# A LayerNorm, attention and MLP block on one core: the MLP's matmuls cut into 32-row pieces, one row group after another

## The chip, the cores and the metric

One core of a Trainium2 chip runs the whole kernel. The metric is the device time of one execution in microseconds (us): the median of three runs before the change is 1019.53 us (1019.48 to 1019.62). The core has a matrix engine (TensorE, PE in the profile, its weight loads PEld), a vector engine (VectorE, DVE), a scalar engine (ScalarE, ACT), GpSimd (POOL) and SyncE (SP), which issues most DMA transfers. Matmuls write into PSUM, here eight banks of 128 x 512 float32. Each engine works through its own queue in order and waits for others on semaphores.

## The reference, cut to what matters

```python
xn = _layernorm(x)                               # x: 2048 x 448
q = (xn @ wq).reshape(B, S, 16, 28)              # 16 heads of 28
k, v = xn @ wk, xn @ wv                          # one head of keys and values for all
p = softmax(einsum("bhqd,bkd->bhqk", q, k) * 28 ** -0.5)
o = einsum("bhqk,bkd->bhqd", p, v) @ wo
y = max(xn @ w1, 0) @ w2                         # w1: 448 x 1792
return x + o + y
```

Everything is float32. A product is made of rounded high parts and the remainders (low parts), three matmuls for each step of the contraction.

## The kernel before

The 2048 rows of x are four blocks of 512 (`QB`). The first stage, up to 61.72 us, normalizes and transposes x, projects queries, keys and values, and stores the queries to DRAM (`qscr`). At its end SyncE stores the last block's queries, reads v back in eight gathers into `vt`, after GpSimd's memset of it (L431, L436), and loads queries (L428).

**The MLP stage** (61.72 to 386.90 us) runs over seven parts of 256 hidden columns and the four blocks. A part and a block make two up tiles (`up`, 11 matmuls of 128 rows by 128 x 512 columns into one bank, L559) and four down tiles (`down`, 6 matmuls of 128 by 128 x 448, L573): 56 up and 112 down tiles. An up tile ends with a relu on ScalarE (`hH`, L562) and a remainder on VectorE (`hL`, L563), a down tile with VectorE adding the bank to `acc` (L579). `load_part` brings a part's weights by four DMAs of SyncE (L180 to L223), and `split_part` makes high and low parts of them on GpSimd in two passes of 1920 columns (L232, L233).

**The maxima.** A softmax needs an upper bound of each row's scores. For each of 16 units of work `u` (a block of queries and four heads) `max_mm` makes 64 score tiles of 128 queries by 512 keys with the high parts alone (L470), and VectorE takes each tile's maximum (L473): 1024 in all. A head has 28 dimensions, so such a matmul takes only 32 rows of the array; four heads lie in four row groups, whose matmuls run side by side into four banks. `max_rows` later transposes a unit's maxima and puts them into the query tile by four DMAs (L495).

**The attention stage** runs from there to the end. `burst` issues the score matmuls of some (mostly four) heads' key blocks, three per score tile (L528), with maxima of later units ahead and behind; ScalarE takes the exponential (L531), `pv` multiplies by v (L596), and `o_proj` tiles (L636) add the output projection.

What sets the order is the text `ORDER`, written out by hand: `F11,3` begins the next MLP tile in bank 3 with 11 steps, `B0.0011223..5612073` is a burst of no scores with maxima on the row groups 0, 0, 1, 1, 2, 2, 3 in the banks named, `V1` a multiplication by v, `R0` a call of `max_rows` with bank 0. So in the MLP stage whole-array matmuls alternate with 53 bursts of maxima, 344 in all, and 680 maxima follow in the attention stage.

Of the kernel before, what the change touches and what calls it, by code (L numbers as in the profile page):

```python
# [17 lines left out]
NU = NQB * NHG  # L18
P_BUFS = 24

# [6 lines left out]

ORDER = """
    F11,3 F6,4 B0.0011223..5612073 f5 F11,5 F6,6 B0.0011223..1207345 f5 F6,1 F6,2 F6,0 F3,7
    B0.002233..345612 f3 F11,0 F5,3 B0.0011233..4561270 f6 F6,4 F6,5 F6,6 F4,1 B0.023..270 v3456 f2 F5,2  # L30
    B0.0012233..3457601 f6 F11,3 F6,4 F3,5 B0.0112233..7601234 f3 F6,7 F6,6 F11,0 F3,1 B0.001123..234576
    f8 F6,0 F6,2 F3,3 B0.0112233..4576102 f3 F6,4 F11,5 F5,7 B0.002233..610234 f6 F6,5 F6,6 F6,1 F3,0
    B0.0011223..2347561 f3 F11,2 F8,3 B0.0011233..4756102 f3 F6,4 F6,7 F6,5 F6,6 F5,1 R0
    B0.001123..234756 f6 F9,0 B0.002233..234756 f2 F6,1 F6,2 F6,3 F6,4 F2,7 B0.112233..560123 f9 F7,4
    B0.0011233..5601237 f4 F6,5 F6,6 F6,0 F6,1 F1,2 B0.001123..374560 f10 F6,1 B0.0012233..3745602 f5
    F6,3 F6,7 F6,4 F3,5 B0.001133..602137 f3 F11,4 F5,6 B0.0112233..0213754 f6 F6,0 F6,2 F6,1 F6,3 F3,7
    B0.0012233..5460213 f8 F10,5 B0.002233..460213 f1 F6,7 F6,4 F6,6 F6,0 F4,2 B0.0011223..1357460 f7
    F11,1 F6,3 B0.001123..574602 F6,1 F6,3 F6,5 F6,7 B0.0011233..4602135 f5 F11,4 F6,6 F3,0
    B0.0012233..2135746 f3 F6,2 F6,1 F9,3 B0.001123..574602 f2 F11,1 F6,5 B0.001133..746023 F6,1 F6,5
    F6,7 F6,4 B0.0112233..6023157 f5 F11,6 F3,0 B0.001123..231574 f3 F6,6 F6,2 F6,3 F7,1  # L40
    B0.0011223..5740623 f4 F11,5 F6,7 F6,4 F3,0 B0.0011233..6231574 f3 F6,6 F11,2 F8,3
    B0.0112233..1574062 f3 F6,1 F6,5 F6,7 F5,4 B0.001123..062315 f1 F11,7 F7,0 B0.0012233..6231547 f4
    F6,6 F6,2 F6,3 F6,1 F4,5 B0.0112233..4706231 f7 F9,4 B0.001123..706231 f2 F6,5 F6,7 F6,0 F6,6 F2,2
    B0.002233..314570 f9 F7,6 B0.0012233..3145702 f4 F6,3 F6,1 F6,4 F5,5 B0.001123..702631 f1 F11,4 F7,7
    B0.0112233..0263154 f4 F6,0 F6,2 F6,6 F6,3 F4,1 B0.0112233..5470263 f7 F11,5 F6,4 F6,7 F3,0
    B0.0011233..2631547 f3 F6,2 F11,6 F5,3 B0.0011223..1547026 f6 F6,1 F6,5 F6,4 F6,7 B0.112233..026315
    F11,4 F8,7 B0.0112233..0263154 f3 F6,0 F6,2 F6,6 F5,3 B0.002233..154702 f1 F11,6 F8,1
    B0.0112233..5470236 f3 F6,5 F6,4 F6,7 F6,0 F3,2 B0.001123..361547 f8 F6,0 B0.001123..361547 f5 F6,2
    F6,3 F4,6 B0.112233..154702 f2 F6,3 F11,1 F6,5 B0.0011223..4702631 f5 F6,4 F6,7 F6,0 F4,2
    B0.112233..631547 f2 F6,0 F6,6 F6,3 F6,1 B6.223..547206317 B7.022.013.5240635143210 V1  # L50
    B4.3.02.6514032 V1 B4.13.0.4635210 V1 B4.3.12.6453021 V1 B4.13.2.3624150 V1 B3.00.0.634201 V1
    B4.2.01.5630412 V1 B5.13.011.3516204536 R1 V1 B4.123..5230461 V1 B3.000..253406 V1 B4.3.12.1250364
    V1 B4.3.02.0162453 V1 B4.03.1.2051364 V1 B6.23.2.201543612 V1 B3.11.1.054236 V1 B3.00.0.150346 V1
    B4.1.23.2154063 V1 B4.13.0.1265340 R2 V1 r B4.3.12.1560342 V2 B4.13.2.0145263 V1 n B4.2.01.1054326
    V1 B4.3.12.5120643 V1 B4.3.12.0541326 V1 B4.3.02.1025643 V1 B4.3.12.5140326 V1 B4.3.02.0521643 V1
    B4.3.12.1045326 V1 B4.03.2.5120643 V1 B4.00.3.5102364 V1 B4.03.2.5130426 V1 B4.13.2.5103642 V1
    B4.23.1.1530264 R3 V1 B4.3.12.1054263 V1 r B4.3.01.4160352 V1 B4.3.02.0415623 V1 n B4.3.12.5024316
    V1 B4.3.01.4510623 V1 B4.23.0.0425316 V1 B4.13.2.2054631 V1 B4.23.0.0245163 R4 V1 B4.3.01.0523164 V1
    B4.23.0.3065421 V1 B4.02.1.6350142 V1 B4.23.0.6350214 R5 V1 B4.3.01.6034215 V1 B5.2.12.46105321 V1
    B3.02.1.462015 V1 B4.12.0.3462051 V1 B4.13.2.4362105 V1 r B4.23.1.3426510 V1 B4.3.01.2364051 V1 n  # L60
    B4.03.1.4253160 V1 B4.12.0.4235016 V1 B4.12.0.2435601 V1 B4.22.3.4235160 V1 B4.3.01.3412506 V1
    B4.3.02.2304615 V1 B4.3.01.4213506 V1 B4.3.02.3402615 V1 B4.03.2.2314506 V1 B4.3.02.2341650 V1
    B4.2.01.1253046 V1 B4.03.12.51426305 V1 B4.13.0.2140653 V1 B4.02.1.1204365 V1 r B4.13.2.1204536 V1
    B4.3.01.2140653 V1 n B4.23.1.0251346 V1 B4.13.2.5012634 V1 B4.12.0.0521463 R5 V1 B4.3.01.0213465 V1
    B4.3.01.3062514 V1 B4.3.02.2310465 V1 B4.3.12.0263514 V1 B4.02.1.3012465 V1 B4.2.01.3012546 V1
    B4.02.1.1340625 V1 B4.3.01.1340652 V1 B4.03.1.0153246 V1 B4.11.00.01356241 V1 B4.3.02.6034512 V1 r
    B4.3.12.4610235 V1 B4.03.2.0436512 V1 n B4.1.0.046325 O12,1 B4.3.02.4056321 V1 B4.13.2.6420153 V1
    B4.02.1.4602315 V2 B4.13.2.4602531 R6 V1 B4.2.01.4201536 V1 B4.13.2.0432615 V1 B4.03.1.4023561 V1
    B4.23.0.4032156 R3 V1 B4.2.01.4206153 V1 B4.3.02.0452361 V1 B4.03.1.2064153 V1 B4.0.1.204631 O12,5
    O5,2 r B4.02..014635 f7 O2,0 B4.1.0.146352 f10 n B4.13.2.4126350 V2 B4.012..1462035 V2  # L70
    B4.23.1.1240635 V1 B4.02.1.4102563 V1 B4.23.0.4102356 V1 B4.3.12.0421635 V1 B4.13.2.1034526 V1
    B4.03.2.0143652 V1 B4.12.0.0134265 V1 B4.13.2.1034526 V1 B4.23.1.0143652 V1 B4.3.01.4031265 R1 V1
    B4.2.01.4605321 V2 B4.12.0.0426153 V1 B4.3.02.4026315 r V1 B4.2.01.6410523 V1 B4.13.2.1624305 V1 n
    B4.3.12.6142530 V1 B4.3.02.2631045 V1 B4.3.02.1246530 V1 B4.3.12.6132045 V1 B4.13.2.2641530 V1
    B4.3.12.6214503 V1 B4.3.02.4602135 V1 B4.3.01.2436501 V1 B4.3.02.6204135 V1 B4.3.12.4632501 V1
    B4.03.1.2406135 V1 B4.11.3.2460513 V1 B4.03.2.4256301 V1 B4.23.1.4265130 R6 V1 r B4.2.01.4520136 V1
    B4.23.1.2435601 V1 n B4.03.2.3254160 V1 B4.13.0.3245016 V1 B4.03.1.2354601 V1 B4.00.3.2345160 V1
    B4.12.0.2314056 V1 B4.1.0.321460 V1 B4.1.0.523014 V1 B4.3.02.6254301 V1 B4.2.01.4602153 V1
    B4.13.2.0456321 V1 B4.2.01.4065312 V1 B4.12.3.6410253 V1 B4.3.01.4610325 V1 B4.23.0.0426513 V1 r
    B4.2.01.2064351 V1 B4.12.0.6250143 R2 V1 n B4.3.01.6503142 V1 B4.13.2.3645201 V1 B4.3.02.6354120 V1  # L80
    B4.3.02.4623051 V1 B4.3.01.3456120 V1 B4.23.1.6324051 V1 B4.3.12.2643105 V1 B4.13.2.3206541 V1
    B4.2.01.2360154 V1 B4.23.0.6253401 V1 B4.13.2.5632140 V1 B4.1.0.652301 V1 B4.0.2.456123 O12,0 O7,4 r
    B4.0.1.536120 f5 O11,5 n B4.01..306124 f1 O6,3 B4.1.0.601524 f6 B4.3.02.0641523 V2 B4.23.0.1026345
    V1 B4.1.0.216053 V2 B4.123..4123605 V1 B4.3.01.1426305 V1 B4.3.01.6104253 V2 B4.23.0.4651302 V1
    B4.13.2.5416230 V1 B4.13.2.4561023 V1 B4.13.0.5416302 V1 B4.23.1.4561230 V1 B4.1.0.641502 V1
    B4.13.0.3462150 V1 B4.23.0.4326015 V1 B4.13.0.2463501 V1 r B4.3.01.4236150 V1 B4.3.12.6452031 V1 n
# [17 lines left out]
def attention_plus_mlp(ctx: ExitStack, tc: tile.TileContext, x, wq, wk, wv, wo, w1, w2, out):  # L104
# [293 lines left out]
    for b in range(1, NQB):  # L398
# [12 lines left out]
        if b == 2:  # L411
            split_part(0, g0)
# [347 lines left out]
```

## Time and profile before

| what | us |
|---|---|
| median of three runs | 1019.53 |
| the profiled execution, its own time | 1021.57 |
| its span | 1019.8 |
| MLP stage in it | 325.2 |
| VectorE's busy time in the MLP stage | 306.1 |
| first MLP matmul | 61.72 |
| last matmul of the MLP | 386.9 |

A profile's row gives the start and length in us, or for groups the count, busy time, mean length in ns and idle time before; names before the arrow are written, names behind it are read. A matmul's length includes the time until its result is in PSUM, so matmuls overlap, and the pace is read from starts. `L559` is line 559 of the kernel before. In the changed kernel the lines are others: L672 for MLP matmuls, L545 for maxima.

### The profile page before, as it was taken

Reading aid. Unit: us, or ns where it says so; the run is one execution under the profiler, and the core shown is the slowest. Engines: PE = TensorE matmul, PEld = TensorE weight load, DVE = VectorE, ACT = ScalarE, POOL = GpSimd, SP = SyncE. Lnnn points to the kernel's source line nnn. Section 1 sums busy time; section 2 is a strip of 40 time slices with the busy share of each in tenths; the row PEclk is TensorE's granted clock in tenths of the full one; section 3 lists DMA queues with packets and bytes.
Section 4 is the critical chain, followed back from the end, with each engine's and each line's share of the span. In section 5 each row is a group of like instructions: output and inputs, shape, how many; then the busy total and the mean of one; then the engine's idle time right before and its main releaser. Section 6 shows DMA issues by size and latency. Waiting matters only on the chain.

```text
span 1019.8 us, 20214 instructions
## 1 busy us (share of the span) xinstructions
PE 1012.6 (99%) x7964; PEld 602.2 (59%) x7964; DVE 800.0 (78%) x1383; ACT 606.4 (59%) x1185; POOL 114.7 (11%) x109
## 2 busy tenths in 40 slices
PE   9999999999999999999999999999999999999998
PEld 8787777777778775444444455444446444446444
DVE  7659999999999998888788876888886787785402
ACT  5531011100011006888989987889987899897994
POOL 4302202020210002011011011010111010110110
PEclk9999999999999998999999999999999999999999
DMA  7653010100200001001001102000101011000001
GB/s 244 246 168 107 1 50 1 50 1 15 74 1 11 1 11 33 33 13 44 23 23 33 33 22 71 22 23 29 37 14 59 21 33 33 2 13 29 22 13 37
DMA packets 28354, 43.22 MB, mean 42 GB/s; under 512 B 9140, under 2 KB 20084, under 8 KB 28260
## 3 DMA queue, kind: packets, MB, share of 16 engines
q1 hardware_dynamic: 27972, 41.48, 12.6%
q8 instruction: 62, 1.02, 0.4%
q10 hardware_dynamic: 288, 0.46, 0.1%
q14 instruction: 32, 0.26, 0.1%
HBM read 29.36 MB, written 12.18 MB: 41 GB/s over the span
## 4 chain that ended last, share of the span: by engine, by line
PE 97%; DVE 2%; DMA 1%; ACT 0%; SPq 0%; issue 0%; DVEq 0%; ACTq 0%
PE o L596 25%; PE b L528 24%; PE b L559 13%; PE b L573 12%; PE b L470 10%; PE b L636 4%; PE b L346 3%; PE o L559 2%; PE o L573 2%; DVE nmx L473 1%; PE b L355 1%; PE b L295 1%; PE b L324 0%; PE o L470 0%; DMA acc<-in_A_x 0%; DMA d<-oS 0%
## 5 line engine op out<-in xcount | busy, mean ns | idle before, releaser
L473 DVE TENSOR_REDUCE nmx<-b 128x1 f32<-128x512 f32 x980 | 617.6, 684 | 116.1 <-PE b L470 99.6
L531 ACT ACTIVATE p<-b 128x512 f32<-128x512 f32 x1023 | 527.7, 608 | 94.1 <-PE b L528 90.1
L528 PE MATMUL b<-q,kHL 28*128 28x512 f32 x3069 | 341.3, 427 | 0.5 <-DVE nmx L473 0.5
L528 PEld LDWEIGHTS b<-q,kHL 28*128 28x128 f32 x3069 | 202.2, 183 | 182.6 <-DVE nmx L473 129.6
L470 PE MATMUL b<-kHL,qhi 28*128 28x512 f32 x980 | 271.7, 467 | 0.1
L596 PE MATMUL o<-p,vtile 128*32 128x512 f32 x2048 | 269.7, 606 | 0.0
L562 ACT ACTIVATE hH<-b 128x512 fp32r<-128x512 f32 x49 | 29.4, 599 | 230.2 <-PE b L559 214.8
L470 PEld LDWEIGHTS b<-kHL,qhi 28*128 28x128 f32 x980 | 120.4, 183 | 77.0 <-DVE nmx L473 30.1
L559 PE MATMUL b<-xt,w 128*128 128x512 f32 x539 | 135.7, 397 | 0.0
L559 PEld LDWEIGHTS b<-xt,w 128*128 128x128 f32 x539 | 98.8, 188 | 28.1 <-issue 9.1
L573 PE MATMUL b<-w,hH 128*128 128x448 f32 x396 | 114.5, 369 | 0.0
L596 PEld LDWEIGHTS o<-p,vtile 128*32 128x32 f32 x2048 | 42.6, 108 | 74.2 <-issue 68.2
L573 PEld LDWEIGHTS b<-w,hH 128*128 128x128 f32 x396 | 73.2, 188 | 11.3 <-issue 2.9
L620 POOL TENSOR_TENSOR on<-rb,oS 128x512 f32<-128x512 f32 x15 | 19.3, 1285 | 535.3 <-DMA rb<-rscr 431.3
L573 PE MATMUL b<-w,hL 128*128 128x448 f32 x198 | 72.7, 367 | 0.0
L579 DVE TENSOR_TENSOR acc<-b,acc 128x448 f32<-128x448 f32 x99 | 56.8, 613 | 0.8 <-PE b L573 0.6
L573 PEld LDWEIGHTS b<-w,hL 128*128 128x128 f32 x198 | 37.2, 188 | 3.8 <-issue 0.9
L641 DVE TENSOR_TENSOR acc<-b,acc 128x448 f32<-128x448 f32 x16 | 10.0, 624 | 36.7 <-PE b L636 36.6
L563 DVE SCALAR_TENSOR_TENSOR hL<-b,hH 128x512 fp32r<-128x512 f32 x49 | 33.0, 681 | 3.1 <-ACT hH L562 2.9
L232 POOL TENSOR_SCALAR w<-stg 128x1920 fp32r<-128x1920 f32 x7 | 12.6, 1804 | 190.8 <-PE b L573 144.7
L346 PE MATMUL b<-xt,w 128*128 128x512 f32 x132 | 31.2, 391 | 0.0
L233 POOL TENSOR_TENSOR w<-stg,w 128x1920 fp32r<-128x1920 f32 x7 | 30.3, 4328 | 0.6
(107 smaller groups left out, 520.1 us busy)
## 6 DMA issues: line engine op xcount, KB each, us to landing
qscr<-qs SPq DMA_DIRECT2D x16, 512.0 KB
q<-qscr SPq DMA_DIRECT2D x16, 512.0 KB
qhi<-qscr SPq DMA_DIRECT2D x16, 256.0 KB
rb<-rscr SPq DMA_DIRECT2D x60, 64.0 KB
out<-acc SPq DMA_DIRECT2D x16, 224.0 KB
acc<-in_A_x SPq DMA_DIRECT2D x14, 224.0 KB
stg<-in_B_w SPq DMA_DIRECT2D x7, 448.0 KB
stg<-in_B_w SPq DMA_DIRECT2D x7, 384.0 KB
```

Source lines behind the costliest of these rows:

```text
L233: nc.gpsimd.tensor_tensor(wt[:, 1, 0:n], g[:, 0:n], wt[:, 0, 0:n].bitcast(F32), op=ALU.subtract)
L346: nc.tensor.matmul(pq, w, xm, start=n == 0, stop=n == len(steps) - 1)
L470: nc.tensor.matmul(pm, qhi[u][rows, s * P : (s + 1) * P], kHL[rows, h, 0], start=True, stop=True)
L473: nc.vector.tensor_reduce(nmx[u][:, r, s, h : h + 1], pm, axis=AX.X, op=ALU.max)
L528: nc.tensor.matmul(ps[r], kHL[rows, kt, w, keys], qst[u][rows, s, :], start=k == 0, stop=k == 2)
L531: nc.scalar.activation(p, ps[r], AF.Exp, scale=SCALE)
L559: nc.tensor.matmul(ph, w, xm, start=i == 0, stop=i == len(steps) - 1)
L563: nc.vector.scalar_tensor_tensor(hL[:, f], ph, 0.0, hH[:, f].bitcast(F32), op0=ALU.max, op1=ALU.subtract)
L573: nc.tensor.matmul(py[:, 0:D], hm[:, i * P : (i + 1) * P], wm, start=k == 0, stop=k == len(steps) - 1)
L579: nc.vector.tensor_tensor(acc[:, t, :], py[:, 0:D], acc[:, t, :], op=ALU.add)
L596: nc.tensor.matmul(o_acc[u][RB * j : RB * (j + 1)], vtile[:, kb, :], ps[j], start=kb == 0, stop=kb == NKB - 1)
L636: nc.tensor.matmul(py[:, 0:D], om[:, i * P : (i + 1) * P], wm, start=n == 0, stop=n == len(steps) - 1)
```

## The change

The whole contraction of an MLP tile is cut by rows: `Tile.passes(r)` lists the pieces of row group `r` (32 of 128 partitions), 11 or 10 for an up tile (the last chunk of xn's low part needs no second pass on row groups 2 and 3), 6 for a down tile. All four row groups add into the same bank, one after the other. Between two visits stands a hop: the last matmul of a visit is awaited by an instruction on SyncE (`nc.sync.nop()`), and the first matmul of the next visit waits for that one.

So that the row groups work side by side, several tiles are open at once, each visited by another row group. A new text, `ROWS`, gives the order matmul by matmul: a digit is the next matmul of that row group, `a` to `d` open a tile, `e` to `h` take up an open one, `i` to `l` are single maxima, `m` to `p` with `q` to `t` are pairs of maxima, `v` pops a piece of VectorE's work. `ORDER` is left with the attention stage.

Further parts: in a pair, the second matmul takes `kD`, the difference of two key blocks, ScalarE takes its relu into `more`, and VectorE adds the first tile and takes the maximum of both in one pass (`max_combine`). A down tile ends with a ScalarE copy into `y` and a GpSimd addition to `acc`. `split_part` works in six pieces, one per tile begun. `v_rows` transposes v into one bank. The MLP stage makes 426 maxima now (292 single, 67 pairs), the attention stage 598. Its 250 bursts have 22 without maxima where there were 11.

The core of the diff; the order texts are shown by one line:

```diff
-    F11,3 F6,4 B0.0011223..5612073 f5 F11,5 F6,6 B0.0011223..1207345 f5 F6,1 F6,2 F6,0 F3,7
+    a3b4c5012012012012012d6012301230123012313o7m23s1q03f53e41g33012012012vA012012l1vA012012l0012vAp7012
...
+    class Tile:
+        def __init__(self, kind, n, i, b):
...
+            if kind == "U" and i == 0:
+                if blk == 1 and 1 <= p < NPART - 1:
+                    raw[p + 1] = load_part(p + 1)
+                if blk == 2 and p < NPART - 1:
+                    splits.append(split_part(p + 1, raw.pop(p + 1)))
+            if splits and next(splits[0], True):
+                splits.pop()
...
+        def matmuls(self, r):
+            o = self.ps if self.kind == "U" else self.ps[:, 0:D]
+            steps = self.passes(r)
+            for k, (w, m) in enumerate(steps):
+                self.left -= 1
+                mm = nc.tensor.matmul(o, w, m, start=self.left == self.n_mm - 1, stop=self.left == 0)
+                if k == 0 and self.before:
+                    tc.add_manual_dep(mm.ins, self.before, HOP, reason="the row group before is done")
+                if k + 1 == len(steps) and self.left:
+                    seen = nc.sync.nop()
+                    tc.add_manual_dep(seen.ins, mm.ins.name, HOP, reason="the row group is done")
+                    self.before = seen.ins.name
                 yield
...
-        t = blk * TPB + i
-        nc.vector.tensor_tensor(acc[:, t, :], py[:, 0:D], acc[:, t, :], op=ALU.add)
-        yield
...
+            a = acc[:, blk * TPB + self.i, :]
+            y = dpool.tile([P, D], F32, name="y", bufs=4)
+            nc.scalar.activation(y, self.ps[:, 0:D], AF.Copy)
+            nc.gpsimd.tensor_tensor(a, y, a, op=ALU.add)
...
+    def max_combine(u, pm, dst, more):
+        nc.vector.tensor_tensor_reduce(more, pm, more, 1.0, LEAST, ALU.add, ALU.max, dst)
+        n_max[u] += 2
...
+    def owe_combine(a, d):
+        more = dpool.tile([P, QB], F32, name="more")
+        nc.scalar.activation(more, d[1], AF.Relu)
```

TensorE before, at the MLP's first burst (xt and w are the MLP's operands, kHL and qhi the keys and queries of the maxima, b0 to b6 and o the eight banks):

```order
L559 MATMUL b3_783<-xt_198,w_631 128x512 x9
L559 MATMUL b4_797<-xt_198,w_631 128x512 [waits PE_49]
L559 MATMUL b4_797<-xt_198,w_631 128x512 x5
L470 MATMUL b5_805<-kHL_76,qhi_681 128x512 [waits DMAHW7_49,PE_49]
L470 MATMUL b6_808<-kHL_76,qhi_681 128x512
L470 MATMUL b1_811<-kHL_76,qhi_681 128x512 [waits DVE_49]
L470 MATMUL b2_814<-kHL_76,qhi_681 128x512 [waits DVE_49]
L470 MATMUL b0_817<-kHL_76,qhi_681 128x512
L470 MATMUL o_820<-kHL_76,qhi_681 128x512
L470 MATMUL b3_823<-kHL_76,qhi_681 128x512 [waits DVE_49]
L559 MATMUL b4_797<-xt_198,w_631 128x512 x5
```

Whole tiles stand in a row, and seven maxima stand together between two parts of a tile.

TensorE now, at the first hops; the first of these rows is the 38th matmul of the MLP stage (kD is the difference of key blocks):

```order
L672 MATMUL b6_812<-xt_353,w_633 128x512
L545 MATMUL o_838<-kHL_76,qhi_687 128x512 [waits DMAHW7_49]
L545 MATMUL b2_840<-kHL_76,qhi_687 128x512 [waits DVE_49]
L672 MATMUL b6_812<-xt_353,w_633 128x512
L545 MATMUL b1_843<-kD_77,qhi_687 128x512
L545 MATMUL b0_847<-kD_77,qhi_687 128x512
L672 MATMUL b6_812<-xt_353,w_633 128x512
L672 MATMUL b5_795<-xt_353,w_633 128x512 [waits SP_sequencer_49]
L672 MATMUL b6_812<-xt_353,w_633 128x512
L672 MATMUL b4_793<-xt_199,w_633 128x512 [waits SP_sequencer_49]
L672 MATMUL b5_795<-xt_353,w_633 128x512
L672 MATMUL b3_791<-xt_199,w_633 128x512
```

Pieces of four tiles alternate, the maxima stand singly between them, and a tile taken up by its next row group (b5, b4) waits for SyncE.

SyncE before, from the last stores of the first stage on (stg is the staging tile of the MLP's weights):

```order
L334 DMA qscr<-qs 128x1024 x4
L436 DMA q<-qscr 16x1x1024
L436 DMA q<-qscr 12x1x1024
...
L428 DMA q<-qscr 128x1024 x4
L180 DMA stg<-in_B_w 128x3x256
L181 DMA stg<-in_B_w 64x256
L182 DMA stg<-in_B_w 64x256
L223 DMA stg<-in_B_w 128x2x448
L369 DMA qhi<-qscr 128x512
```

SyncE now at the same place; the waiting instructions of the hops are not printed:

```order
L405 DMA qscr<-qs 128x1024 x4
L512 DMA q<-qscr 16x1x1024
L512 DMA q<-qscr 12x1x1024
...
L504 DMA q<-qscr 128x1024 x3
L246 DMA stg<-in_B_w 128x3x256
L247 DMA stg<-in_B_w 64x256
L248 DMA stg<-in_B_w 64x256
L289 DMA stg<-in_B_w 128x2x448
L440 DMA qhi<-qscr 128x512
```

The transfers are the same but for one query load, which comes later. The first 75 hops stand between L504 and L246, behind the gathers and the query loads, and the others stand among the transfers that follow.

More of the change, by code (lines that the diff above doesn't have):

```diff
@@ L467, in max_mm, with max_reduce, max_final @@
             nmx[u] = small.tile([P, HG, TPB, 4], F32, name="nmx", bufs=3)
+            nc.vector.memset(nmx[u], LEAST)
         pm = bank(b)
         rows = slice(RB * r, RB * r + DH)
-        nc.tensor.matmul(
-            pm, qhi[u][rows, s * P : (s + 1) * P], kHL[rows, h, 0], start=True, stop=True
-        )
-        nc.vector.tensor_reduce(nmx[u][:, r, s, h : h + 1], pm, axis=AX.X, op=ALU.max)
-        if any(k and k[0][0] == u for k in todo.values()):
-            return
+        k = kD[rows, h // 2] if keys is kD else kHL[rows, h, 0]
+        nc.tensor.matmul(pm, qhi[u][rows, s * P : (s + 1) * P], k, start=True, stop=True)
+        return u, pm, nmx[u][:, r, s, h : h + 1]
+    def max_reduce(u, pm, dst):
+        nc.vector.tensor_reduce(dst, pm, axis=AX.X, op=ALU.max)
+        n_max[u] += 1
+    def max_combine(u, pm, dst, more):
+        nc.vector.tensor_tensor_reduce(more, pm, more, 1.0, LEAST, ALU.add, ALU.max, dst)
+        n_max[u] += 2
+    def max_final(u):
         nm = small.tile([P, HG, 1, TPB], F32, name="nm")
@@ L566, in down @@
-    def down(n, i, b):
-        p, blk = tasks[n]
-        hH, hL = hid[n]
-        w = parts[p][1]
-        py = bank(b)
-        steps = [(hm[:, f], w[:, wi, f, :]) for f in range(FC) for hm, wi in ((hH, 0), (hH, 1), (hL, 0))]
-        for k, (hm, wm) in enumerate(steps):
-            nc.tensor.matmul(
-                py[:, 0:D], hm[:, i * P : (i + 1) * P], wm, start=k == 0, stop=k == len(steps) - 1
-            )
-            if k + 1 < len(steps):
-                yield
-        t = blk * TPB + i
-        nc.vector.tensor_tensor(acc[:, t, :], py[:, 0:D], acc[:, t, :], op=ALU.add)
-        yield
+    splits = []
@@ new lines, in attention_plus_mlp, with owe_final, owe_reduce, work @@
+    owed, at, busy, first_of = [], {}, {}, {}
+    def owe_final(u):
+        if n_max[u] == HG * TPB * 4:
+            owed.append(lambda: max_final(u))
+    def owe_reduce(*m):
+        def work():
+            max_reduce(*m)
+            owe_final(m[0])
+        owed.append(work)
+    def owe_combine(a, d):
+        more = dpool.tile([P, QB], F32, name="more")
+        nc.scalar.activation(more, d[1], AF.Relu)
+        def work():
+            max_combine(*a, more)
+            owe_final(a[0])
+        owed.append(work)
@@ new lines, in go_on @@
+    def go_on(r):
+        t, mm = busy[r]
+        next(mm)
+        if not t.left:
+            t.finish()
+    stream = iter("".join(ROWS.split()))
+    n_tiles = 0
+    for c in stream:
+        if c in "0123":
+            go_on(int(c))
+            continue
+        b = next(stream)
+        r = (ord(c) - ord("a")) % HG
+        if c in "abcd":
+            at[b] = Tile(*mlp_tiles[n_tiles], b)
+            n_tiles += 1
+        if c in "abcdefgh":
+            busy[r] = at[b], at[b].matmuls(r)
+            go_on(r)
+        elif c in "ijkl":
+            owe_reduce(*max_mm(b, r))
+        elif c in "mnop":
+            first_of[r] = max_mm(b, r)
+        elif c in "qrst":
+            owe_combine(first_of.pop(r), max_mm(b, r, kD))
+        elif c == "v":
+            owed.pop(ord(b) - ord("A"))()
+        else:
+            max_rows(b)
+            v_rows(next(stream))
```

342 lines of the change are left out of this document (209 added, 133 removed).

## The prediction

> **What bounds the kernel now.** I read the page first, then three windows (the MLP stage, the attention stage with row maxima and without), the groups of the MLP stage, and the timeline of single tiles. First the page's head:
>
> ```profile
> span 1019.8 us, 20214 instructions
> ...
> PE 1012.6 (99%) x7964; PEld 602.2 (59%) x7964; DVE 800.0 (78%) x1383; ACT 606.4 (59%) x1185; POOL 114.7 (11%) x109
> ```
>
> TensorE always has a matmul in flight, so time is won by issuing less on it or by issuing more at once. The windows (stretch, length, then busy time and count for PE, PEld, DVE, ACT, POOL, granted clock) split the span:
>
> ```profile
> 61.72:386.90 325.18, 325.18 (x1650) 257.22 (x1648) 306.08 (x527) 35.14 (x62) 39.00 (x14) 1.00 0.09 30
> 398.00:948.00 550.00, 549.36 (x5329) 258.76 (x5323) 432.56 (x716) 475.36 (x934) 45.29 (x40) 1.00 0.09 29
> 948.00:1005.00 57.00, 57.00 (x557) 26.28 (x555) 9.25 (x18) 51.12 (x102) 6.38 (x6) 1.00 0.03 7
> 375.00:400.00 25.00, 24.73 (x156) 15.96 (x153) 20.84 (x35) 9.18 (x19) 5.43 (x3) 0.86 0.15 33
> ```
>
> The MLP stage takes 325.2 us, with TensorE at 100% and VectorE at 306.1 (94%): both are full. What a tile costs there is read from the starts of TensorE's rows:
>
> ```profile
> 207.77 1.56 PE L559 MATMUL o<-xt,w 128*128 128x512 f32 x6
> 209.25 0.79 PE L470 MATMUL b<-kHL,qhi 28*128 28x512 f32 x7
> 209.97 1.42 PE L559 MATMUL o<-xt,w 128*128 128x512 f32 x5
> 211.23 2.66 PE L559 MATMUL b<-xt,w 128*128 128x512 f32 x11
> 213.73 0.57 PE L573 MATMUL b<-w,hH 128*128 128x448 f32 x2
> 214.13 0.36 PE L573 MATMUL b<-w,hL 128*128 128x448 f32 x1
> 214.34 0.36 PE L573 MATMUL b<-w,hH 128*128 128x448 f32 x1
> ```
>
> Eleven up matmuls last 213.73 - 211.23 = 2.50 us, 0.227 each; three down matmuls 214.34 - 213.73 = 0.61, 0.203 each. The stage has 56 x 11 = 616 of the first and 112 x 6 = 672 of the second: 139.8 + 136.4 = 276.2 us. The other 49.0 us go to the 53 bursts with 344 maxima that the order counts there, 0.92 each. The one above agrees: 211.23 - 207.77 = 3.46 for eleven up matmuls and a burst, 0.96 over 2.50, for seven maxima that are two rounds on four row groups. Two rounds are 0.46; the other half is the entry and exit.
>
> **The change: the lanes of the MLP stage.** With every MLP matmul cut into 32-row pieces, a row group ("lane") carries one piece of each: 616 up pieces on lanes 0 and 1 (560 on 2 and 3), 672 down pieces, and 88, 94, 124 and 120 of now 426 maxima. Lane 1 is the fullest: 710 pieces of 512 columns and 672 of 448. At the whole-array prices that is 161.2 + 136.4 = 297.6 us, the low end. For the high end, four lanes at work side by side:
>
> ```profile
> 966.23 1.92 PE L596 MATMUL o<-p,vtile 128*32 128x512 f32 x16
> 968.09 1.74 PE L528 MATMUL b<-q,kHL 28*128 28x512 f32 x21
> 969.75 0.64 PE L596 MATMUL o<-p,vtile 128*32 128x512 f32 x4
> ```
>
> 21 score matmuls put six on a lane in 969.75 - 968.09 = 1.66 us; without an entry and exit of some 0.24 (half the 0.46 above, since this is one switch) that is 0.237 a round, with its waits: 168.3 + 142.4 = 310.7. I take the middle, 0.232 and 0.207: 164.7 + 139.1 = **303.8 us**. The 53 entries and exits are gone, and maxima ride in rounds that the MLP fills.
>
> By the Trainium skill (TensorEngine Tiling (Array Packing), When to Use Tiling) row tiles are for contractions of up to 64; a contraction of 128 fills the array whole, and cutting it should win nothing. The rows above say the same of the matmuls (297.6 is 276.2 plus 94 rounds of maxima), so by rule and row the gain is only the switches.
>
> **The hops.** A group of the MLP stage (mean length 397 ns) and the first row after an up tile on ScalarE:
>
> ```profile
> L559 PE MATMUL b<-xt,w 128*128 128x512 f32 x539 | 135.7, 397 | 0.0
> ```
>
> ```profile
> 213.93 0.60 ACT L562 ACTIVATE hH<-b 128x512 fp32r<-128x512 f32 x1 [1.90 <-PE b L559]
> ```
>
> A tile has four visits, so three hops: 504 hops from TensorE over a SyncE instruction and back. Behind a visit's waiting first matmul stands, in TensorE's one queue, the work of all four lanes. A last matmul is seen 0.40 us after its start, and a waiting engine starts 0.04 after it ends (the last of the eleven, at 211.23 + 10 x 0.227 = 213.50, ends at 213.89, and the relu starts at 213.93); the weight load behind a wait adds what the first of five up matmuls lost above, 1.26 - 5 x 0.227 = 0.12. With two such handovers a hop is about 0.40 + 2 x 0.04 + 0.12 = 0.60, up to 0.70 with SyncE's own step, which no row shows. In the new order the visits of a tile stand 14 matmuls apart in the median, 13 at the first quarter, 11 at the first tenth. 5,466 matmuls in 303.8 us are 0.056 each, so 0.78, 0.72 and 0.61 us: most hops fit and about fifty are short by up to 0.1. With the lanes not quite in step I put **4 us** on both (0 to 17: the order has 1,462 greedy rounds against 1,382 on lane 1, and 80 rounds are 17).
>
> **What stands ahead of the hops on SyncE.** SyncE takes its queue in order, and its DMA issues block hops (start, length, line, what is moved):
>
> ```profile
> 54.90 8.70 SPq L334 DMA_DIRECT2D qscr<-qs  x4
> 67.15 6.42 SPq L436 DMA_DIRECT2D q<-qscr  x8
> 73.62 1.36 SPq L428 DMA_DIRECT2D q<-qscr  x3
> ...
> 138.77 2.82 SPq L495 DMA_DIRECT2D q<-rows  x4
> 141.69 0.38 SPq L180 DMA_DIRECT2D stg<-in_B_w  x1
> ...
> 143.34 0.58 SPq L223 DMA_DIRECT2D stg<-in_B_w  x1
> ```
>
> TensorE's first MLP row and GpSimd's row of that time:
>
> ```profile
> 61.72 4.01 PE L559 MATMUL b<-xt,w 128*128 128x512 f32 x17
> ```
>
> ```profile
> 66.17 0.95 POOL L431 MEMSET q<- 128x1024 f32 x1 [14.78 <-DVE hL L563]
> ```
>
> The MLP starts at 61.72, but SyncE is busy with v's eight gathers, held back by GpSimd's memset until 67.12, and three query loads until 73.62 + 1.36 = 74.98. None moves. The first hop is the 45th matmul, some twelve rounds or 2.8 us in: TensorE stands from 64.5 to 75.1, **10.5 us**, with only four maxima ahead of it. Each of five weight loads in the stage is four issues, 141.69 to 143.92 = 2.2 us; the hop behind is then ready 0.45 + 2.2 + 0.1 after its load's turn, against some 1.6 by the order (the tile's next visit stands 29 matmuls on, at 0.056): 1.1 each, **5.5**. The maxima's rows come once: 0.9 until ScalarE has copied them, 2.8 of issues and one more query load make 4.1, against 31 matmuls or 1.7 to the next hop: **2.5**. An idle TensorE also loses clock: the window 375:400, with its pauses, was granted 0.86, so 0.14 x 25 = 3.5 us were lost; for the first stall I take **2.5** (0 to 3.5).
>
> **What the other engines do.** The accumulation into acc leaves VectorE for a ScalarE copy and a GpSimd add; maxima in pairs take one ScalarE pass and one VectorE pass with a second, short instruction. Rows:
>
> ```profile
> L473 DVE TENSOR_REDUCE nmx<-b 128x1 f32<-128x512 f32 x301 | 187.5, 682 | 12.7 <-PE b L470 11.1 <-PE o L470 1.2
> L563 DVE SCALAR_TENSOR_TENSOR hL<-b,hH 128x512 fp32r<-128x512 f32 x49 | 33.0, 681 | 3.1 <-ACT hH L562 2.9
> L562 ACT ACTIVATE hH<-b 128x512 fp32r<-128x512 f32 x49 | 29.4, 599 | 230.2 <-PE b L559 214.8 <-DVE nmx L473 15.4
> L233 POOL TENSOR_TENSOR w<-stg,w 128x1920 fp32r<-128x1920 f32 x6 | 26.0, 4330 | 0.5
> L232 POOL TENSOR_SCALAR w<-stg 128x1920 fp32r<-128x1920 f32 x6 | 10.8, 1804 | 190.8 <-PE b L573 144.7 <-DMA stg<-in_B_w 46.1
> ```
>
> VectorE: 292 single maxima at 187.5/301 = 0.62, 56 hL at 33.0/49 = 0.67, 67 pairs at 0.67 plus up to 0.2 for the second instruction: 181 + 38 + 58 = 277 us, under 306. The pair's instruction is in no row; 0.67 is the nearest (PSUM and SBUF in, 512 columns), twice that is the far end (322). ScalarE: (56 + 67 + 112) x 0.60 = 141. GpSimd: 448 columns at 4.33/1920 us each are 1.0, so 112 x 1.0 + 37 for the splits (26.0 + 10.8) = 149. Both lie beside TensorE's 304 at no cost; if GpSimd fell behind, the four y buffers would hold ScalarE's copy and with it a PSUM bank. The smaller edits (kD on GpSimd, v's transposes in one bank, ksel and tmp in another pool) lie beside other work: nothing.
>
> Stage: 303.8 + 4 + 10.5 + 5.5 + 2.5 + 2.5 = 328.8 against 325.2: **+3.6 us**.
>
> **Attention.** It keeps 598 maxima instead of 680. With maxima it issues 5,329 matmuls in 550.0 us, 0.103 each; almost without, 557 in 57.0, 0.102. So one matmul less is worth 0.103: 82 x 0.103 = 8.4, the likely low end (0 if ScalarE's exponentials set the pace, which at 475 of 550 they nearly do). If each spared a round, 82 x 0.232 = 19. I take **-11**, near the first, because 22 bursts instead of 11 now have no maxima and lose a round.
>
> Sum: 3.6 - 11 = -7.4. The profiled execution took 1021.57 with a span of 1019.8; this makes it 1014.2. On the median 1019.53 it gives **1012 us**; its own range, with lanes and attention between their nearer values, is 1003 to 1020.
>
> **Rivals.**
> SyncE is not in the way (0.20): the hops are served between the DMA issues. Then 10.5 + 5.5 + 2.5 + 2.5 = 21 us fall away: 991. Against it stand the SyncE rows; for it, that the gathers' 6.4 us were measured with nothing waiting behind.
>
> Issue becomes the bound (0.22). One more row on the score bursts:
>
> ```profile
> 964.27 2.03 PE L528 MATMUL b<-q,kHL 28*128 28x512 f32 x21
> ```
>
> 5,466 weight loads and matmuls need one pair per 0.056 us for 300 us. No row shows that pace held: the 37 from 964.27 to 968.09 took 0.103 each, the best burst 1.66/21 = 0.079, both within the array's own time. For the change, the seven maxima above went in 0.72 with a switch in it. The rival decides at (325.2 + 11 - 25)/5466 = 0.057 us (25 being the 4 and 21 us of loss and stalls), just above what is needed. At 0.062, a quarter of the way from 0.056 to 0.079, the lanes take 339 instead of 308 and the kernel 1012 + 31 = 1043; at 0.079 it would be far slower. The Trainium skill (TensorE: Matmul & The Clock Gate, Wait — 56ns, not 53.3ns?) gives some 62 ns per matmul where microcode decodes, and a floor of about 25 between starts where it does not bind; by the first this rival is certain, by the second void, and no row here tells which holds.
>
> VectorE or PSUM banks hold it (0.11): at twice the price VectorE needs 322, and SyncE's 21 us of stalls come on top, 343 in the stage: +18 - 11, 1027.
>
> **How the numbers follow.** The forecast has 0.47 (0.42 of it faster). Faster by over 0.2% (2 us, about what a measurement here can tell from no change) is below 1017.5: that 0.42 and the first rival, 0.62. Within: 0.06. Slower: 0.32, the second and third rival but for 0.01. The range goes from 988 (the first rival with its lanes at the low end) to 1044.
>
> **What would show it.** In the changed profile: TensorE idle from about 64.5 to 75 with SyncE as releaser, and a clock below 1.00 after it; about 1.1 us at each weight load; otherwise rounds of 0.23 with four lanes in flight; VectorE at 85%; the MLP stage's end near 390, attention 622 us long. A first hop before 70 makes the first rival right; lane rounds over 0.24 with no releaser the second. No idle time at the first hops, or an attention stage that keeps its 633 us, would make the sum wrong.

## The result, and the profile after

The changed kernel takes 1032.28 us (median of four runs, 1030.32 to 1034.15) against 1019.58 for the kernel before on the same chip: a ratio of 1.0124, 95% interval 1.0099 to 1.015. The forecast was 1012, faster; it came out slower by 12.7 us, inside the range (988 to 1044) and on the other side of no change. The profiled execution took 1034.06 with a span of 1031.9.

The head of the page of the changed kernel:

```profile
span 1031.9 us, 28533 instructions
...
PE 1006.4 (98%) x11704; PEld 639.8 (62%) x11704; DVE 717.8 (70%) x1287; ACT 699.6 (68%) x1361; POOL 248.9 (24%) x251
```

VectorE went from 800 to 718 us busy, as meant, and TensorE still has a matmul in flight for 98% of the span. The busy share alone shows little of the loss: TensorE is busy as long as one lane of four has a matmul in flight, and a halved clock is hidden altogether. The windows show both. First the whole MLP stage, most of attention, and the stretches in which something is wrong (length, then busy time and count for PE, PEld, DVE, ACT, POOL, then the granted clock):

```profile
61.95:404.05 342.10, 323.94 (x5473) 307.00 (x5472) 268.36 (x504) 127.66 (x235) 165.66 (x147) 0.98 0.10 30
404.05:964.00 559.95, 558.19 (x5355) 253.07 (x5355) 399.12 (x662) 486.50 (x958) 53.56 (x47) 0.98 0.10 30
66.00:76.50 10.50, 0.00 (x0) 0.00 (x0) 1.31 (x4) 1.09 (x2) 0.95 (x1) 0.58 0.18 50
76.50:82.00 5.50, 5.47 (x45) 5.42 (x49) 1.38 (x2) 0.37 (x1) 2.28 (x3) 0.56 0.75 276
405.00:420.00 15.00, 14.75 (x98) 7.09 (x94) 10.66 (x18) 10.13 (x21) 7.78 (x7) 0.66 0.31 72
458.00:468.00 10.00, 8.64 (x58) 3.35 (x58) 5.95 (x10) 5.33 (x11) 3.16 (x3) 0.66 0.10 28
```

The MLP stage takes 342.1 us (325.2 before, 328.8 forecast), what follows it 1031.9 - 404.05 = 627.9 (632.9 before, 622 forecast). So both halves missed: +13.3 and +5.9. The 404.05 takes in two maxima behind the last MLP matmul, which starts at 403.52; counted to that start, as the 325.2 before is and as the stages of the experiments below are, the stage is 341.6.

Where the first stall sits is in three views. TensorE's row (start, length; in brackets the idle time and its releaser), the first behind a matmul that started at 64.84:

```profile
76.53 2.07 PE L672 MATMUL b<-xt,w 32*128 32x512 f32 x12 [11.30 <-SPq L676]
```

SyncE's DMA issues of that time, and GpSimd's rows:

```profile
55.09 8.64 SPq L405 DMA_DIRECT2D qscr<-qs  x4
68.58 6.42 SPq L512 DMA_DIRECT2D q<-qscr  x8
75.05 1.37 SPq L504 DMA_DIRECT2D q<-qscr  x3
```

```profile
59.81 1.29 POOL L484 TENSOR_TENSOR kD<-kHL 128x512 fp32r<-128x512 f32 x1 [7.41 <-ACT kHL L397]
67.61 0.95 POOL L507 MEMSET q<- 128x1024 f32 x1 [6.51 <-DMA qscr<-qs]
```

This is the mechanism of the forecast, row by row: the first hop (L676) stands behind eight gathers that wait for a memset, and three query loads, to 75.05 + 1.37 = 76.4; TensorE goes on 0.1 later. It is 11.7 us where 10.5 were forecast, because the memset, which waits for the last qscr write to land, ran 1.4 later than before (67.61 against 66.17).

Then the pace between the pauses, in windows of the MLP stage (length, TensorE busy and its count, clock, DMA share, GB/s):

```profile
61.95:100.00 38.05, 26.73 (x372) 0.82 0.21 73
100.00:125.00 25.00, 25.00 (x445) 1.00 0.01 2
125.00:150.00 25.00, 23.28 (x403) 1.00 0.18 52
150.00:175.00 25.00, 25.00 (x436) 1.00 0.01 3
175.00:200.00 25.00, 23.62 (x412) 1.00 0.17 52
200.00:225.00 25.00, 23.82 (x415) 1.00 0.10 22
225.00:250.00 25.00, 25.00 (x451) 1.00 0.08 23
250.00:275.00 25.00, 24.21 (x420) 1.00 0.17 51
275.00:300.00 25.00, 25.00 (x445) 1.00 0.01 3
300.00:325.00 25.00, 24.59 (x422) 1.00 0.17 53
325.00:350.00 25.00, 25.00 (x438) 1.00 0.01 2
350.00:375.00 25.00, 25.00 (x440) 1.00 0.04 13
375.00:404.05 29.05, 27.69 (x456) 1.00 0.06 21
```

Six windows are without a pause: 2,655 matmuls in 150 us. A matmul that lies across an edge counts in both windows (the thirteen count 5,555 for 5,473), so about 7 come off each, and a matmul takes 150/2,613 = 0.0574 us. By that pace the stage's 5,466 matmuls are 314 us, and the rest is what each window lost: 38.05 - 365 x 0.0574 = 17.1 at the start, 8.1 in the five windows with a weight load, 3.3 in the last one with the maxima's rows. 314 + 17.1 + 8.1 + 3.3 = 342.5, and 342.1 were measured. The 8.1 hold 6.5 us of pauses at the loads and two pauses of 0.8 that VectorE releases, shown next.

One load, on TensorE and on SyncE, shows what the others repeat:

```profile
127.66 0.35 PE L672 MATMUL b<-w,hL 32*128 32x448 f32 x1
129.32 0.47 PE L672 MATMUL b<-w,hH 32*128 32x448 f32 x1 [1.31 <-SPq L676]
```

```profile
126.96 0.39 SPq L246 DMA_DIRECT2D stg<-in_B_w  x1
127.40 0.54 SPq L247 DMA_DIRECT2D stg<-in_B_w  x1
127.99 0.59 SPq L248 DMA_DIRECT2D stg<-in_B_w  x1
128.62 0.59 SPq L289 DMA_DIRECT2D stg<-in_B_w  x1
```

The four issues end at 129.21, and every lane stands still until 129.32: starts 1.66 apart. The five pauses are 1.66, 1.34, 1.57, 1.15 and 0.80 us. Two more of 0.8, at 145 and 195, have VectorE as releaser, where a unit's last maxima are put together between reduces.

The groups of the other engines (busy time, mean ns of one, idle time ahead and its releasers) that answer to the costs in the forecast:

```profile
L549 DVE TENSOR_REDUCE nmx<-b 128x1 f32<-128x512 f32 x859 | 550.7, 685 | 181.4 <-PE b L545 129.5 <-PE b L612 28.5 <-PE b L672 18.5
L553 DVE CUSTOM_DVE_ANT_0 more<-b,more 128x512 f32<-128x512 f32 x55 | 37.6, 686 | 17.3 <-ACT more L714 17.0
L696 ACT ACTIVATE y<-b 128x448 f32<-128x448 f32 x98 | 52.4, 545 | 95.3 <-PE b L672 83.6 <-PE o L672 7.2 <-PE b L545 2.9
L697 POOL TENSOR_TENSOR acc<-y,acc 128x448 f32<-128x448 f32 x112 | 127.7, 1152 | 158.9 <-ACT y L696 158.5
```

A pair's pass is 0.69 us, no dearer than a single reduce; VectorE is busy for 268 of 342 us; GpSimd idles 159 us for lack of copies. None of them is full; how far they set the pace all the same, the runs below test.

### The profile page after: what moved, and what is told of

Read it like the earlier page. It is cut to its first block, busy times and chain, and to the rows that moved or that the text cites. A ratio compares the mean times of both kernels' runs of the same rounds, so it can differ in the third digit from the quotient of the medians.

```text
span 1031.9 us, 28533 instructions
## 1 busy us (share of the span) xinstructions
PE 1006.4 (98%) x11704; PEld 639.8 (62%) x11704; DVE 717.8 (70%) x1287; ACT 699.6 (68%) x1361; POOL 248.9 (24%) x251
## 3 DMA queue, kind: packets, MB, share of 16 engines
q1 hardware_dynamic: 27972, 41.48, 12.7%
## 4 chain that ended last, share of the span: by engine, by line
PE 93%; SPq 2%; DVE 2%; DMA 1%; ACT 1%; issue 1%; POOL 0%; POOLq 0%; DVEq 0%; ACTq 0%
PE b L612 24%; PE o L769 24%; PE b L672 22%; PE b L545 8%; PE b L809 4%; PE o L672 3%; PE b L417 3%; PE b L426 1%; PE b L366 1%; SPq L512 1%; DVE nmx L549 1%; PE o L545 0%; PE b L395 0%; DMA d<-oS 0%; DMA qscr<-qs 0%
## 5 line engine op out<-in xcount | busy, mean ns | idle before, releaser
L612 PE MATMUL b<-q,kHL 28*128 28x512 f32 (+1 forms) x3066 | 335.0, 429 | 1.4 <-DVE nmx L549 1.3
L612 PEld LDWEIGHTS b<-q,kHL 28*128 28x128 f32 (+1 forms) x3066 | 194.4, 185 | 198.6 <-DVE nmx L549 101.3
L672 PE MATMUL b<-xt,w 32*128 32x512 f32 x2058 | 304.2, 397 | 12.7 <-SPq L676 12.7
L672 PE MATMUL b<-w,hH 32*128 32x448 f32 x1568 | 282.2, 368 | 3.9 <-SPq L676 3.9
L672 PEld LDWEIGHTS b<-xt,w 32*128 32x128 f32 x2058 | 248.0, 185 | 15.4 <-SPq L676 13.5
L672 PE MATMUL b<-w,hL 32*128 32x448 f32 x784 | 211.3, 363 | 0.0
L672 PEld LDWEIGHTS b<-w,hH 32*128 32x128 f32 x1568 | 205.4, 183 | 8.8 <-SPq L676 5.5
L697 POOL TENSOR_TENSOR acc<-y,acc 128x448 f32<-128x448 f32 x112 | 127.7, 1152 | 158.9 <-ACT y L696 158.5
L672 PEld LDWEIGHTS b<-w,hL 32*128 32x128 f32 x784 | 123.0, 183 | 0.4
L672 PE MATMUL o<-xt,w 32*128 32x512 f32 x294 | 73.8, 391 | 0.0
```

What stands on the lines that cost most here:

```text
L612: nc.tensor.matmul(ps[r], kHL[rows, kt, w, keys], qst[u][rows, s, :], start=k == 0, stop=k == 2)
L672: mm = nc.tensor.matmul(o, w, m, start=self.left == self.n_mm - 1, stop=self.left == 0)
L697: nc.gpsimd.tensor_tensor(a, y, a, op=ALU.add)
```

## The experiments

Theory: what was lost is TensorE standing behind SyncE's queue, plus the clock that follows. Rivals: PSUM banks and VectorE; ScalarE or GpSimd; the issue of 5,466 small matmuls. All times are medians, with the ratio to the kernel before and its 95% interval.

**Gathers off SyncE.** In load_q and at the gathers (L504 to L516), with a list that the MLP loop empties:

```diff
-            nc.sync.dma_start(vt[d0 : d0 + n].rearrange("p s q -> p (s q)"), src)
-    load_q(0); load_q(1); load_q(2)
+            later.append((vt[d0 : d0 + n].rearrange("p s q -> p (s q)"), src))
...
+            if later and n_tiles % 6 == 0:
+                one_later()          # nc.scalar.dma_start of the next one
```

> Edit: v's eight gathers and the first three query loads leave SyncE's queue; each is issued by ScalarE on its own, one at every sixth tile of the MLP stage. Everything else is as in the changed kernel. Theory (SyncE's queue blocks the first hops): the stall from 64.84 to 76.53 (11.7 us) goes, and with it the half clock behind it (76.5 to 81.4 at half is 2.4 us lost) and the slow rounds of the restart: 14 to 16.5 us in all, 1032.3 to about 1017. Rival 1 (something else holds TensorE there, PSUM banks or VectorE's hL): no more than 4 us, 1028 to 1033. Rival 2 (a DMA issue on ScalarE holds a PSUM bank as long as it held a hop on SyncE): eleven times about 0.5 us come back, 1021 to 1023.

Measured: 1019.19, ratio 0.9993 (0.9973 to 1.0013). The 11.7 us pause is gone and the kernel 13 faster than changed: the theory's side. In the profile the stage is 8.5 shorter (333.1 against 341.6), not 14 to 16.5: the clock is still at half twice inside the stage, 3.4 us each (from 69.5 and from 380.1), and 1.4 us of pause stay at 66.2, released by a pair's ScalarE copy, which itself waited:

```profile
66.90 1.09 ACT L721 ACTIVATE more<-b 128x512 f32<-128x512 f32 x2 [4.31 <-DMA qscr<-qs]
```

**Loads off SyncE.** In load_part:

```diff
+        by = nc.scalar if p > 1 else nc.sync
-            nc.sync.dma_start(...)   # four of them
+            by.dma_start(...)
```

> Edit: the five weight loads of the MLP stage (four DMAs each) are issued by ScalarE instead of SyncE; the rest is as in the changed kernel, the stall at the start too. Theory (the issues hold the hop behind them): the pauses of 1.66, 1.34, 1.57, 1.15 and 0.80 us and the rounds lost around them go, 6 to 8 us of 1032.3: about 1025. Rival (the pauses come from GpSimd's splits of the weights or from a late ScalarE copy, not from SyncE): 1031 to 1034.

Measured: 1032.0, ratio 1.0119 (1.0099 to 1.0138): no gain. The time went to the rival's side, and its profile says why. ScalarE and TensorE at the same load:

```profile
127.91 0.60 ACT L688 ACTIVATE hH<-b 128x512 fp32r<-128x512 f32 x1 [0.68 <-PE b L673]
127.92 0.39 ACTq L246 DMA_DIRECT2D stg<-in_B_w  x1
...
129.56 0.60 ACTq L290 DMA_DIRECT2D stg<-in_B_w  x1
130.21 0.60 ACT L688 ACTIVATE hH<-b 128x512 fp32r<-128x512 f32 x1 [1.70 <-PE b L546]
130.70 0.98 ACT L697 ACTIVATE y<-b 128x448 f32<-128x448 f32 x2
131.29 0.50 PE L546 MATMUL b<-kHL,qhi 28*128 28x512 f32 x1 [1.06 <-ACT y L697]
```

The same 2.2 us of issue now shut ScalarE, whose copies free the PSUM banks, and TensorE waits for a bank (ACT y) instead of a hop. The stall was moved.

**All of the stage's DMAs off SyncE.** Both edits, and in load_qhi and max_rows:

```diff
-            nc.sync.dma_start(qhi[u].bitcast(F32), queries(u)[:, 0])
+            mlp_q[0].dma_start(qhi[u].bitcast(F32), queries(u)[:, 0])   # nc.scalar in the MLP stage
```

> Edit: both of the edits before, and the queries' loads and the maxima's four row DMAs of the MLP stage are ScalarE's too: SyncE has nothing but hops between the start and the end of the stage. Theory: the start's 14 to 16.5, the loads' 6 to 8 and some 2 us at the maxima's rows add up, 1032.3 - 25 = about 1007 (1004 to 1011), below the kernel before (1019.5). Rival (lanes, banks or VectorE hold the stage, and the stalls hid their lateness): no more than half of it, 1018 or above.

Measured: 1021.67, ratio 1.0018 (1.0003 to 1.0033): the start's gain and nothing more, and the theory's 1007 missed. At the maxima's rows the pause grew from 1.75 to 2.84 us, for the reason just seen.

**No reduces in the MLP stage.**

```diff
-            max_reduce(*m)
+            n_max[m[0]] += 1
...
-        nc.scalar.activation(more, d[1], AF.Relu)
-            max_combine(*a, more)
+            n_max[a[0]] += 2
```

> Edit: the row maxima of the MLP stage keep their matmuls, but are not reduced: 292 single reduces, 67 ScalarE copies and 67 pair instructions are left out (a constant stands in for those maxima). SyncE's stalls stay. Theory (lanes and order set the pace between the stalls: 1,462 rounds, 0.057 us per matmul): the stage stays at 335 to 342 us, the kernel 1025 to 1032. Rival (VectorE, or PSUM banks that it frees late, set the pace): the stage falls to lane 1's 297.6 plus some 25 us of stalls, 323, the kernel to about 1013.

Measured: 1028.63, ratio 1.0073 (1.0047 to 1.0099); the stage 336.9, of 335 to 342 forecast by the theory. VectorE costs 4.7 us of the stage (341.6 to 336.9), the two pauses at its final maxima among them; it is not the bound. Between the pauses a matmul takes 0.0564 us here (five windows of 25 us with 2,252 matmuls, less 7 each), against 0.0574.

**One issue at a time.** As the first experiment, and:

```diff
+    spread = []      # load_part and unit 0's max_rows append their four DMAs here
...
             n_tiles += 1
+            if spread:
+                nc.scalar.dma_start(*spread.pop(0))
```

> Edit: as e1_start, and the four DMAs of each weight load and the four row DMAs of the maxima are no longer issued in one go: ScalarE issues one of them per tile. Theory (what costs is a queue, SyncE's or ScalarE's, that is shut for 2.2 us at a stretch; a single issue of 0.4 to 0.6 us fits into the slack of a PSUM bank): of the 6.5 us lost around the five loads some 5 go and 2 at the maxima's rows, e1_start's 1019.2 to about 1012 (1010 to 1015). Rival (any issue on an engine that frees banks costs its own length, however it is spaced): 1018 to 1020, as e1_start.

Measured: 1011.61, ratio 0.9914 (0.989 to 0.9937): faster than the kernel before by 0.86%, and than the first experiment by 7.6 us. The same work, on the same engine as in the second experiment, one issue per tile instead of four in a row, costs next to nothing in the windows:

```profile
100.00:125.00 25.00, 25.00 (x445) 24.32 (x443) 21.92 (x40) 9.19 (x17) 10.27 (x9) 1.00 0.15 44
200.00:225.00 25.00, 25.00 (x452) 24.26 (x448) 20.63 (x38) 9.71 (x18) 14.16 (x14) 1.00 0.27 84
```

Both windows hold a weight load or other spread transfers (DMA shares 0.15 and 0.27) and run at the pace of the pause-free ones; the five others with such transfers hold 429 to 438 matmuls, where the changed kernel's pause-free ones hold 436 to 451. The stage is 322.9. Single executions at a clock of 1.000 say the same as the medians: 1014.75 for the first experiment, 1007.12 for this one.

**One issue at a time on SyncE.** The first experiment with nc.sync in place of nc.scalar in its edit.

> Edit: as e1_start, the eight gathers and three query loads one at every sixth tile, but issued by SyncE, between its hops. Theory (a hop takes about 0.6 us and its distance is 0.78 in the median, so 0.8 us of issue ahead of it is late by some 0.5): 8 x 0.6 + 3 x 0.2 = 5 us over e1_start's 1019.2, 1023 to 1025. Rival (single issues hide between the hops; only the lump of 7.9 us behind a late memset hurt): 1019 to 1020.

Measured: 1020.0, ratio 0.9997 (0.9981 to 1.0013), the same as on ScalarE (1019.19), stage 331.5. My theory of a 0.5 us loss per issue falls: a single issue of up to 0.8 us hides between hops. What hurt was the lump. Only the gathers and query loads were spread on SyncE; the weight loads were not.

**The clock.** The changed kernel again, unedited.

> The changed kernel once more, unedited, for its own times beside the granted clock of each execution. Theory (the halved clock is part of the loss, in pieces of 3.4 us that depend on when a pause falls): times from 1028 to 1035, lower where the clock is higher, by about 10 us for 0.01 of clock, and 1016 to 1018 when carried on to a clock of 1.00. Rival (the differences have another cause): no such line.

Measured: 1030.73, ratio 1.0105 (1.0089 to 1.0122); four executions from 1030.49 to 1032.32 at clocks of 0.988 to 0.986. Too narrow to draw a line by itself; the first experiment's ten executions draw it: 1014.75 at a clock of 1.000, 1016.46 at 0.998, 1018.96 at 0.994, 1022.0 at 0.992, 1023.4 at 0.990. That is 8.8 us for 0.01; the ten executions of e6_spaced_on_sync give 9.2 by the same fit, those of e3_no_sync_dma 7.1. Carried on by 8.8, the changed kernel's 1030.5 at 0.988 would be 1020 at 1.000. But part of its half clock falls into the first stall, where TensorE stands anyway: in this run's profile the halves with work in them cost 2.6 us behind the stall and 5.1 from 409.0, which leaves 1023. Both are estimates, and neither is the 1016 to 1018 expected: by them the changed kernel would not beat the 1019.5 before at full clock either. The kernel before has the same two faces: 1019.5 at 1.000, 1022.4 at 0.996. What a halved clock does is seen in one piece of program, behind the boundary to attention, in this run and in e2_loads:

```profile
409.00:419.20 10.20, 10.20 (x58) 4.23 (x56) 6.79 (x12) 5.66 (x12) 3.03 (x3) 0.50 0.43 106
```

```profile
411.60:422.00 10.40, 10.29 (x99) 4.50 (x101) 8.51 (x16) 9.30 (x21) 3.48 (x3) 1.00 0.48 105
```

58 matmuls against 99 in the same time, and TensorE is "busy" in both.

**Filling the boundary.** As e5_spread, and in the first bursts (the condition takes in seven, with 33 matmuls more, where the text below has eight and 34):

```diff
+                if k == 1 and n_bursts < 8:
+                    nc.tensor.matmul(ps[r], zero[rows], kHL[rows, kt, 0], start=False, stop=False)
```

> Edit: as e5_spread, and in the first eight score bursts of attention each score tile gets one more matmul, with a zero weight, between its second and third (34 in all; nothing is changed in the result). Theory (the clock is halved behind the boundary because TensorE is too little used in the 5 us from 385 to 390, where it waits for ScalarE): the stretch of 13.7 us at half goes, clock 0.997 or more, e5_spread's 1011.6 to 1006 to 1009. Rival (the boundary's waits are for PSUM banks, and 34 more matmuls at 0.06 to 0.1 us only delay them, or the use that counts is not a few matmuls more): clock 0.993 as before, 1012 to 1015.

Measured: 1014.46, ratio 0.9927 (0.9899 to 0.9956); clocks of 0.991 to 1.000 in six executions, the profiled one with 17.1 us at half from 388.9. The rival's side by the number, but a weak test: only five of the 33 had started when the half began. That they cost something isn't shown either: 1014.46 and 1011.61 lie within each other's scatter, and at a clock of 1.000 the two kernels took 1007.93 and 1007.12.

**Lanes alone.** e5_spread with the reduces left out as above.

> Edit: e5_spread and e4_no_reduce together: single DMA issues on ScalarE, and the maxima of the MLP stage are not reduced (a constant stands in for them). What is left of the MLP stage is the lanes. Theory (lanes out of step lose against 294.7 us of full lanes, whatever VectorE does): e5_spread's stage of 322.9 falls by the 4 to 5 us that e4_no_reduce won, to 318, the kernel to about 1007. Rival (with the stalls gone the banks and VectorE are the next bound): the stage falls to 305 or less, the kernel to 994.

Measured: 1001.88, ratio 0.9823 (0.9804 to 0.9843), stage 315.7. The stage fell by 7.2, not by 18: nearer to the theory, a little beyond it. With VectorE nearly empty the pace is the same as ever:

```profile
100.00:125.00 25.00, 25.00 (x449) 24.54 (x443) 2.99 (x5) 8.47 (x16) 11.49 (x11) 1.00 0.15 44
325.00:350.00 25.00, 25.00 (x444) 24.31 (x441) 5.44 (x10) 7.73 (x15) 10.85 (x10) 1.00 0.04 12
```

So most of the 0.057 us per matmul belongs to the lanes, their order and the hops, not to VectorE's reading of the banks. These three aren't separated by any run, and ScalarE's copies still read banks here.

## Why the forecast was wrong

Every wait of the sum was found at its place and with its releaser: the mechanism of SyncE's queue held. The sizes were short, nearly all to the same side, and a gain forecast at 7.4 us had no room for that. The step that failed is the adding up of the losses, and in it two terms above all: the lanes and hops, taken at 307.8 us where 314 were measured, and the clock, for which the sum took 2.5 us at one place and attention nothing, where 5.1 us more were lost:

- **Clock, the term left out of attention.** "For the first stall I take 2.5" counted one place. The profiled execution ran at half from 76.5 to 81.4 (2.4 lost: there the step held), for 10.2 us from 409.0 and for 6.8 us from 460.2. At half, those two are 5.1 + 3.4 = 8.5 us against 6.8/2 = 3.4 before. So 5.1 us were unforecast, and they are what attention lacked: 627.9 - 632.9 = -5.0, or -10.1 without them, beside -11 forecast. The price of 0.103 per maximum was right: (559.95 - 8.5)/5,355 is 0.103 again. Some of this is the luck of one execution: a second profile of the changed kernel (a1_again) has no half at 460.2, and from the last MLP matmul's start on it takes 625.7 us against 628.4. The forecast also overlooked a wait in attention, 0.6 us ahead of that second stretch:

```profile
458.79 0.25 DVE L784 RECIPROCAL r<-d 128x16 f32<-128x16 f32 x1 [2.54 <-issue]
459.64 0.50 PE L612 MATMUL b<-q,kHL 28*128 28x512 f32 x2 [1.27 <-DVE nmx L549]
```

  VectorE stands for 2.5 us ahead of a reciprocal (the four DMAs for its operand `d` were issued from 452.7 to 455.1), and TensorE for 1.3 behind the reduces that follow. In the profile before, no such wait of TensorE is over 0.3; seven of the nine other profiles of the new order have one of 0.7 to 1.3, and only in e2_loads did a half clock (3.4 us) follow it.
- **Lanes and hops:** 303.8 + 4 forecast, 314 measured, inside the bounds that were given (to 320.8) and 6 over the value chosen. Where the 6 come from is shown only in part: without the reduces the pace makes 308 us in e4_no_reduce (0.0564 x 5,466) and 312 in e8_spread_no_reduce (0.0571), so 2 to 6 us of it are VectorE's. What holds the rest isn't settled. The order's 1,462 rounds at 297.6/1,382 each would be 315, close to the 314; but the row groups don't keep strictly to such rounds (last section), so that may be luck. The hops' own part looks small: from 82 us on, TensorE's weight loading stood idle for a hop nine times, six of them at the load pauses and the maxima's rows (0.84 to 1.79 us), the others 0.13 or less.
- **First stall:** 17.1 us with its clock, against 13. Of the 4 us, 1.2 are the later memset, and the rest are slow rounds after the restart (82 to 100 us); that the engines' buffers fill again there is a reading, not shown. e1_start still loses some 6 us up to 100, 1.4 of them its pause and 1.7 its half clock.
- **Weight loads:** 6.5 against 5.5. **Maxima's rows:** 3.3 against 2.5, with the stage's end. **VectorE:** two pauses of 0.8, against nothing, though it was forecast busy for 277 of 329 us (268 of 342 measured).

Added up: 6 + 4.1 + 1 + 0.8 + 1.6 in the stage is 13.5 (13.3 measured), and 5.1 + 0.9 in attention (the wait at 459.64 is as long as this rest; that it is the same isn't shown); with 0.4 more outside the span, that is the 20 us from the 1014.2 forecast for a profiled execution to 1034.06.

The rivals: "SyncE is not in the way" is refuted by the rows and by e1_start. "Issue becomes the bound" as well, as it was priced, at 0.062 and more: the six windows hold 0.0574 per matmul, the fastest hundred in a row (from 82 us on) go at 0.0527, and half of all matmuls start within 0.045 us of the one before. This settles the rule that the forecast set beside the rows, 62 ns a matmul where microcode decodes (the Trainium skill, TensorE: Matmul & The Clock Gate, Wait — 56ns, not 53.3ns?): it would make 339 us of the lanes, and 314 were measured. "VectorE or PSUM banks" has 4.7 to 7.2 us in it, not 18.

What stays open is why the clock falls behind the boundary so often. The profile before shows it there for 6.8 us, from 391.6 on; those of the new order for 6.8 (e4_no_reduce), 10.2 (the changed kernel twice, e1_start, e3_no_sync_dma, e8_spread_no_reduce), 13.7 (e5_spread, e6_spaced_on_sync) and 17.1 us (e7_filler), yet not at all in e2_loads, whose rows in the 5 us ahead of it are the same. TensorE is thinly used there: 37 matmuls in the 4.95 us ahead of 409.0, 0.134 each, and 38 in e2_loads. The Trainium skill (TensorE: Matmul & The Clock Gate, What's actually happening) has a free-running window of 3.4 us; the lengths here, 3.4, 6.8, 10.2, 13.7 and 17.1, are multiples of it, and a start that moves against such a window would explain two outcomes for one program. That it takes an idle window to lose the clock, as that page's table of states has it, doesn't fit: in the 5 us ahead of 409.0 TensorE's longest pause was 0.23 us.

## What to carry to other kernels

When an idle sequencer is made a relay between an engine and itself, a lump in its queue can become a stall of that engine, as the eight gathers and the weight loads did here; moving the weight loads' lumps to another engine that frees buffers only moved the stall, while the same DMAs issued there one per tile cost next to nothing (1032 to 1011.6 us with the gathers spread too). Look for a halved clock at every place where the profile before has one, and not just behind the longest pause. Where a gain is the difference of several terms, take each of them at the bound that the order gives, not at the best row.

## What the runs showed that was not expected

- Matmuls of different row groups start out of queue order. Ahead of the first hop the queue ends with two pairs of maxima, for row groups 2 and 0, and behind the last of them an up matmul of row group 3. The order has 40 up matmuls ahead of the hop; the trace has all 40 started by 64.37, and three of the four maxima after that:

```profile
64.36 0.39 PE L545 MATMUL o<-kHL,qhi 28*128 28x512 f32 x1
64.37 0.39 PE L672 MATMUL b<-xt,w 32*128 32x512 f32 x1
64.60 0.39 PE L545 MATMUL b<-kD,qhi 28*128 28x512 f32 x1
64.60 0.39 PE L545 MATMUL b<-kHL,qhi 28*128 28x512 f32 x1
64.84 0.39 PE L545 MATMUL b<-kD,qhi 28*128 28x512 f32 x1
```

  Here a busy row group doesn't hold the others back; a semaphore wait does, and holds all four for 11.7 us. So TensorE's queue is not worked through strictly in order, as the first section has it of each engine.
- A hop costs 0.09 us beside the matmul itself: SyncE's event comes 0.031 after the matmul's end (the median of 504 hops) and lasts 0.017, and where a weight load had waited for it, it follows 0.043 after that (the commonest value; many loads come later, in their turn). With the 0.39 of a matmul that is 0.48 us to the weight load, against the 0.60 to 0.70 of the forecast, which took 0.12 more for the load; the ends of matmuls are modelled in the profile.
- A clock at half shows as full busy time: 58 matmuls in 10.2 us, TensorE 100% busy.
